# A gated linear attention kernel on one core: later loads for the third group, w_in's upper half in two units, and another order of the steps around two groups

## Chip, core and metric

The kernel runs on one core of one Trainium2 chip. The metric is the device time of one execution in microseconds (us). Before the change it was 279.6 us, the median of three runs (279.18 to 279.66). The engines are called PE (TensorE), DVE (VectorE), ACT (ScalarE), POOL (GpSimd) and SP (SyncE, which here only issues DMAs).

## What is computed

There are two parts, one behind the other. The first is a recurrence for each of 4 batches and 8 heads, over 768 positions, with a 48 x 48 state that decays row by row:

```
state = alpha[t][:, None] * state + outer(k[t], v[t])
y[t]  = q[t] @ state
```

The 8 heads side by side give x (4 x 768 x 384). The second part projects x with w_in (384 x 1024) into a value half and a gate half, runs a first-order scan over the positions on the value half (`h = a * h + val[t]`, with a from A_log), multiplies it by silu of the gate, and projects with w_out (512 x 384) to the output. The weights and A_log come as 64-bit floats and are converted on the core; all the rest is float32.

## The kernel before

The work is cut into 12 groups of 256 positions: 4 batches of 3 groups. A group of the recurrence is called m here, as in the code, and a group of the second part n; in the loop over n the second part of group n runs beside the recurrence of group m = n + 1, and DVE prepares group n + 2 or later. Everything is under a manual schedule: each engine runs its instructions in the order of the program text, waits by semaphores where it needs another's result, and nothing is moved by a planner. So the order of calls in the loop is the order on every engine.

For one group of the recurrence:

- `load_raw`, `load_steps` (L401, L418) load q, k and alpha, `load_v` (L431) loads v. All loads behind the first ones are issued on SP's queue, in order. For the first four groups `load_steps` uses one half of a buffer per group; from then on `load_raw` fills the whole buffer.
- The inputs are turned so that positions run along the free axis. For the first groups PE does it (`turned`, L684: by matmuls with an identity or, for k and q of group 1 and alpha of group 3, by transposes) and ACT copies the result (`alphas`, `straighten`). From group 4 on DVE does it by `turn` (L594).
- DVE forms running products of alpha, P (`scan_P`, L625) and V (`scan_V`, L642), and from them Zk and Zq (`scaled_k`, L609; `scaled_q`, L602). From group 4 on these steps are a generator, `products` (L656): turn of alpha, P, turn of k, V, Zk, turn of q, Zq, seven steps; `go(count)` in the loop runs the next `count` of them.
- `first(m)` is `scores` (L733: 64 small matmuls of Zk with Zq on PE) and `masks` (L748: DVE masks one half of the result into A, ACT copies the other into AK, from group 3 on POOL masks AK).
- `second(m)` is `values` (L766) and `states` (L795) on PE, and `add_up` (L820), which adds the states up on POOL; for the first groups `add_banks` (L832) does it on DVE.
- `third(m)` is `carried` (L782) and `values` again on PE, and `join` (L900): ACT copies y and DMAs bring it into the layout xT of the second part.

For one group of the second part, `project(n, cc)` (L915) is called for cc = 0 to 3: six matmul calls into two PSUM banks, first the value half, then the gate half; the scan over positions on DVE; silu on ACT; and a function that multiplies both (on DVE for n < 2, on POOL later). `output(n)` (L945) multiplies by w_out, ACT copies the result (L950) into one of two buffers, and SP stores it. PSUM banks for `project`, `output` and half of `scores` are taken in turn from four, in pairs, so that each pair is used again two calls later.

The weights: `load_w` (L451) loads a unit of w_in's column blocks, `low(i)` (L539) and `convert(i)` (L546) bring block i into float32 with one step on ACT, two on DVE and one on POOL; blocks 4 and 5 are the halves of w_out. `units` (L447) has three units: block 0, block 1, and blocks 2 and 3 together.

The opening (L962 to L1029) runs group 0 and issues the loads. At L1001 POOL writes one element of the alpha buffer; the load of alpha for group 2 behind it must wait for that write, and so must all SP issues after it. Then follow the unit of blocks 2 and 3, k and q of group 2, alpha of group 3, v of group 1, w_out and v of group 2.

Of the kernel before, what the change touches and what calls it, by code (L numbers as in the profile page):

```python
# [346 lines left out]
def fast(  # L347
# [96 lines left out]
    w_ins = [const.tile([C, NK, 2, C], FP32, name=f"w_in{i}") for i in range(NI)]  # L444
    NW = 6
    UW = NK * 2 * C
    units = [range(0, 1), range(1, 2), range(2, 4)]  # L447
    wbits = {us: const.tile([C, NK, 2, len(us) * C, 2], U32, name=f"wbits{us.start}") for us in units}
    wobits = [const.tile([C, 2, DM, 2], U32, name=f"wobits{i}") for i in range(2)]

# [225 lines left out]
    def bank(tag=None):  # L676
        if tag:
            return ps_at.tile([C, 512], FP32, tag=tag, name=tag)
        return ps_mm.tile([C, 512], FP32, tag="mm", name="mm")
# [1 line left out]
    def bank_pair(tag=None):  # L681
        return [bank(tag and f"{tag}{i}") for i in range(2)]

    def turned(m, name, js, t):  # L684
        raw = steps_of(name, m)
        tp = t[:, 0:len(js) * C].rearrange("p (j x) -> p j x", j=len(js))
        if (m, name) in ((1, "k"), (1, "q"), (3, "a")):
            for n, j in enumerate(js):
                nc.tensor.transpose(tp[:, n], raw[:, ds(ROW + j * D - 64, C)], ident)  # L689
                nc.tensor.transpose(tp[0:64, n], raw[:, ds(j * D, 64)], ident)  # L690
            return tp.rearrange("p j (c h) -> p h c j", h=4)
        for n, j in enumerate(js):
            for i in range(2):
                nc.tensor.matmul(tp[ds(64 * i, 64), n], raw[:, ds(i * ROW + j * D, 64)], ident,  # L694
                                 start=True, stop=True, skip_group_check=True)
        return tp.rearrange("p j (c h) -> p h c j", h=4)

    def copy_turned(to, js, tp, engine=None):
        place = by_runs(to)[:, :, :, js.start:js.stop]
        if engine:  # L700
            return engine.tensor_copy(out=place, in_=tp)
        return nc.scalar.activation(place, tp, AF.Copy)

    def turn_over(m, name, to, tags=(None, None)):
        size = NJ // len(tags)
        copies = []
        for n, tag in enumerate(tags):
            js = range(size * n, size * (n + 1))
            copy = copy_turned(to, js, turned(m, name, js, bank(tag)), nc.vector if n % 2 and tag else None)
            if tag:  # L710
                for other in copies[(n + 1) % 2::2]:
                    tc.declare_no_dep(copy.ins, other.ins, reason="the copies write different steps")
                copies.append(copy)
# [198 lines left out]
    prev_h = [None] * NI  # L912
    fs = {}

    def project(n, cc, late=False):  # L915
        if cc == 0:
            if n == 0:
                fs[n] = [wide[:, k // 2, ds(k % 2 * GC, GC)] for k in range(NI)]
            else:
                fs[n] = [f_last[:, k] for k in range(NI)]  # L920
        xT = xTs[n]
        pv, pg = [t[:, 0:GC] for t in bank_pair()]
        order = [(vg, kk) for vg in range(2) for kk in range(NK)]
        if n == 0 and cc == 0:
            order.sort(key=lambda x: x[1])
        for vg, kk in order:
            nc.tensor.matmul((pv, pg)[vg], w_ins[cc][:, kk, vg, :], xT[:, kk, :],  # L927
                             start=(kk == 0), stop=(kk == NK - 1))
        hh = p2.tile([C, GC], FP32, tag=f"h{cc}", name="hh")

        def scan():
            nc.vector.tensor_tensor_scan(  # L932
                out=hh, data0=a_dec[:, cc:cc + 1].to_broadcast([C, GC]), data1=pv,
                initial=prev_h[cc][:, GC - 1:GC] if n % NG else 0.0, op0=ALU.mult, op1=ALU.add)
            prev_h[cc] = hh

        if not late:
            scan()
        sg = p2.tile([C, GC], FP32, tag="sg", name="sg")
        nc.scalar.activation(sg, pg, AF.Silu)  # L940
        engine = nc.vector if n < 2 or n == N - 1 else nc.gpsimd
        f = lambda: engine.tensor_mul(fs[n][cc], sg, hh)  # L942
        return (scan, f) if late else f
# [34 lines left out]
    def go(count):  # L978
        for _ in range(count):
            next(steps, None)  # L980
# [17 lines left out]
    low(0)  # L998
    parts = [turned(1, "q", js, bank()) for js in halves]
    convert(0)  # L1000
    nc.gpsimd.memset(raws["a"][0:1, 0:1], 0.0)  # L1001
    load_steps("a", 2, [nc.sync])
    load_w(units[2], nc.sync)
    masks(0)
    low(1)
    first_values(True)
# [6 lines left out]
    last = P[:, :, GC]  # L1013
    nc.scalar.activation(ratio[:, 0], last, AF.Copy, scale=1.0 / FIRST_PRODUCT)
    nc.scalar.activation(lower[:, :, 0], last, AF.Copy)
    for name in "kqa":
        load_steps(name, 2 + (name == "a"), [nc.sync])
    load_v(1, nc.sync)
    P = scan_P(1)
    first_carried((1,))  # L1020
# [2 lines left out]
    first_join()  # L1023
    nc.scalar.activation(a_dec, a_log, AF.Exp)
    nc.scalar.activation(spare, minus, AF.Silu)
    for half in range(2):
        load_w_out(half, nc.sync)
    load_v(2, nc.sync)
    junk(0)  # L1029

# [11 lines left out]
    def third(m):  # L1042
        if m < N:
# [4 lines left out]
            if m >= NG:  # L1048
                add_up(m, (3,))

    for n in range(N):
        m = n + 1
        if n == 0:
            V = scan_V(1, P)
            f0 = project(n, 0)
            scaled_k(1, tk, V)
            scaled_q(1, tq, P)
            low(2)
            f1 = project(n, 1)
            convert(2)  # L1060
            alphas(2)
            low(3)
            first(m)
            f0()
            f1()
            tk = straighten(2, "k")
            load_raw("k", 3, nc.sync)
            P = scan_P(2)
            tq = straighten(2, "q")
            V = scan_V(2, P)  # L1070
            convert(3)
            junk(1)
            low(4)
            f2 = project(n, 2)
            values(m, True)
            st = states(m)
            add_banks(m, st)
            alphas(3)
            third(m)
            for name in "qa":  # L1080
                load_raw(name, 3 + (name == "a"), nc.sync)
            load_v(3, nc.sync)
            for c in range(G):
                scaled_k(2, tk, V, c)
                scaled_q(2, tq, P, c)
        elif n == 1:
            scores(m)
            h3, f3 = project(0, 3, True)
            masks(m)
            f2()  # L1090
            P = scan_P(3)
            h3()
            values(m, True)
            st = states(m)
            add_banks(m, st)
# [24 lines left out]
            scaled_q(3, tq, P)  # L1120
            f3()
            go(1)
        else:
            if n == 2:
                first(m)
                go(1)
                f0 = project(n, 0)
                second(m)
                go(2)
            else:  # L1130
                second(m)
                go(4)
                f0 = project(n, 0)
            f0()
            load_raw("k", n + 3, nc.sync)
            load_raw("a", n + 3, nc.sync)
            go(1)
            f1 = project(n, 1)
            f1()
            if n == N - 2:  # L1140
                for i in range(0, 2):
                    check_w(i)
            go(1)
            f2 = project(n, 2)
            f2()
            load_raw("q", n + 3, nc.sync)
            if n == N - 2:
                check_w(2)
            if n == N - 1:
                check_flag()  # L1150
            go(1)
            f3 = project(n, 3)
            f3()
            third(m)
            first(m + 1)
            load_v(m + 2, nc.sync)
        if n == N - 2:
            for i in range(3, NW):
                check_w(i)
            check_end()  # L1160
        if n == N - 1:
            tc.mark_branch_hint_location("last", hint=0, engines=[mybir.EngineType.PE, mybir.EngineType.Activation, mybir.EngineType.DVE, mybir.EngineType.SP, mybir.EngineType.Pool])
            value = nc.values_load(flag[0:1, 0:1], min_val=0, max_val=1)
        if 0 < n < N - 1:
            output(n)
    return value


# [59 lines left out]
```

## Time and profile before

| | |
|---|---|
| runs | 279.6, 279.66, 279.18 us |
| the profiled execution | 279.43 us, span 277.7 us |
| granted TensorE clock | 1.0 |
| PE, DVE, POOL, ACT busy | 268.8, 218.3, 122.4, 108.6 us |
| share of PE in the chain that ended last | 92% |
| DMA | 41.18 MB, mean 148 GB/s |

The profiled execution is one run of its own, and the terms of a sum taken from its rows are to be set against its 279.43 us. "Busy" is the time in which an engine had an instruction running. The chain that ended last is found by going back from the last instruction, at each step to what released it; what is on it set the end, and what is not on it had time to spare. In a row of the timeline the first number is the start in us from the begin of the span, the second the length; what stands in brackets behind it is the idle time of the engine before it and the instruction that ended it. L numbers are lines of the kernel.

### The profile page before, as it was taken

Reading aid. Unit: us, or ns where it says so; the run is one execution under the profiler, and the core shown is the slowest. Engines: PE = TensorE matmul, PEld = TensorE weight load, DVE = VectorE, ACT = ScalarE, POOL = GpSimd, SP = SyncE. Lnnn points to the kernel's source line nnn. Section 1 sums busy time; section 2 is a strip of 40 time slices with the busy share of each in tenths; the row PEclk is TensorE's granted clock in tenths of the full one; section 3 lists DMA queues with packets and bytes.
Section 4 is the critical chain, followed back from the end, with each engine's and each line's share of the span. In section 5 each row is a group of like instructions: output and inputs, shape, how many; then the busy total and the mean of one; then the engine's idle time right before and its main releaser. Section 6 shows DMA issues by size and latency. Waiting matters only on the chain.

```text
span 277.7 us, 9598 instructions
## 1 busy us (share of the span) xinstructions
PE 268.8 (97%) x4056; PEld 217.0 (78%) x4056; DVE 218.3 (79%) x281; ACT 108.6 (39%) x244; POOL 122.4 (44%) x141
## 2 busy tenths in 40 slices
PE   7999999999989999899999999999999999999995
PEld 5988887876678688488688688688688688787874
DVE  7979998898798995995895995996995993079540
ACT  2577763461332532341542433433434425213111
POOL 8141223130068574563473584484384476435000
PEclk9999999999999999999999999999999999999999
DMA  6949993845919777487468587576687501201201
GB/s 196 295 140 309 296 262 78 205 88 139 267 48 238 149 199 182 103 214 163 103 181 199 114 205 164 130 197 155 152 186 159 144 0 27 77 1 33 71 5 59
DMA packets 51599, 41.18 MB, mean 148 GB/s; under 512 B 27360, under 2 KB 49536, under 8 KB 51552
## 3 DMA queue, kind: packets, MB, share of 16 engines
q1 hardware_dynamic: 48752, 37.50, 53.1%
q0 software_dynamic: 1408, 2.03, 2.8%
q10 hardware_dynamic: 1392, 0.99, 1.2%
q8 instruction: 33, 0.54, 0.9%
q14 instruction: 14, 0.11, 0.2%
HBM read 32.54 MB, written 4.72 MB: 134 GB/s over the span
## 4 chain that ended last, share of the span: by engine, by line
PE 92%; DVE 3%; DMA 1%; POOL 1%; issue 1%; ACT 1%; SPq 0%; DVEq 0%; ACTq 0%
PE mm L927 45%; PE mm L956 21%; PE y L791 4%; PE y L778 4%; PE mm L744 3%; PE s L744 3%; PE s L810 3%; PE mm L694 2%; PE mm L1189 2%; DMA raw_a<-in_alpha_dram 1%; POOL AK L762 1%; DVE P L630 1%; DVE V L649 1%; PE mm L689 1%; PE y L862 1%
## 5 line engine op out<-in xcount | busy, mean ns | idle before, releaser
L927 PE MATMUL mm<-xT,w_in 128*128 128x256 f32 x576 | 128.9, 382 | 0.6 <-ACT xT L884 0.6
L927 PEld LDWEIGHTS mm<-xT,w_in 128*128 128x128 f32 x576 | 108.1, 190 | 16.3 <-issue 0.8
L956 PE MATMUL mm<-w_out,f_last 128*128 128x384 f32 x160 | 54.1, 492 | 1.3 <-DVE A L759 1.3
L940 ACT ACTIVATE sg<-mm 128x256 f32<-128x256 f32 x48 | 18.4, 384 | 85.8 <-PE mm L927 80.3
L956 PEld LDWEIGHTS mm<-w_out,f_last 128*128 128x128 f32 x160 | 29.7, 190 | 21.1 <-issue 1.4
L830 POOL TENSOR_TENSOR sum<-sum,dS 128x192 f32<-128x192 f32 x30 | 33.2, 1108 | 27.3 <-PE mm L927 13.5
L942 POOL TENSOR_TENSOR f_last<-sg,hh 128x256 f32<-128x256 f32 x36 | 30.9, 862 | 30.6 <-ACT sg L940 23.1
L932 DVE TENSOR_TENSOR_SCAN hh<-a_dec,hh,mm 128x256 f32<-128x256 f32 x32 | 23.4, 732 | 15.4 <-PE mm L927 15.2
L630 DVE TENSOR_TENSOR_SCAN P<-al,lower 128x1028 f32<-128x1028 f32 x12 | 31.1, 2595 | 0.6
L649 DVE TENSOR_TENSOR_SCAN V<-al,ends 128x1028 f32<-128x1028 f32 x12 | 28.3, 2356 | 0.4
L907 POOL DMA_DIRECT2D xT<-yst x40 | 20.5, 517 | 13.1 <-ACT yst L904 11.8
L950 ACT ACTIVATE o_sb<-mm 128x384 f32<-128x384 f32 x22 | 10.8, 491 | 38.4 <-PE mm L956 38.4
L762 POOL TENSOR_TENSOR AK<-AK,mask 128x512 f32<-128x512 f32 x9 | 13.2, 1464 | 17.2 <-ACT AK L760 17.2
L759 DVE TENSOR_TENSOR A<-s,mask 128x256 f32<-128x256 f32 x9 | 3.8, 425 | 21.5 <-PE s L744 21.5
L557 POOL TENSOR_TENSOR w_in<-w_in,wr 128x768 int32<-128x768 int32 x4 | 7.3, 1826 | 26.0 <-DVE wr L555 17.0
L595 DVE STREAM_TRANSPOSE k<-raw_k 128x1024 f32<-128x1024 f32 x9 | 18.3, 2033 | 0.0
L595 DVE STREAM_TRANSPOSE q<-raw_q 128x1024 f32<-128x1024 f32 x9 | 18.2, 2022 | 0.0
L778 PEld LDWEIGHTS y<-AK,v 64*64 64x64 f32 x352 | 12.1, 134 | 6.4 <-issue 5.0
L595 DVE STREAM_TRANSPOSE al<-raw_a 128x1024 f32<-128x1024 f32 x8 | 16.3, 2041 | 0.1
L778 PE MATMUL y<-AK,v 64*64 64x64 f32 x352 | 14.5, 221 | 1.0 <-POOL AK L762 1.0
L791 PEld LDWEIGHTS y<-Zq,sum 48*64 48x64 f32 x656 | 11.8, 134 | 4.3 <-issue 4.1
L791 PE MATMUL y<-Zq,sum 48*64 48x64 f32 x656 | 14.4, 221 | 0.6 <-issue 0.6
(158 smaller groups left out, 392.2 us busy)
## 6 DMA issues: line engine op xcount, KB each, us to landing
v<-in_v_dram SPq DMA_DIRECT2D x22, 192.0 KB, 3.3
out_dram<-o_sb SPq DMA_DIRECT2D x22, 192.0 KB, 2.1
raw_k<-in_k_dram SPq DMA_DIRECT2D x18, 184.0 KB, 3.4
raw_q<-in_q_dram SPq DMA_DIRECT2D x18, 184.0 KB, 3.8
raw_k<-in_k_dram SPq DMA_DIRECT2D x18, 176.0 KB, 3.8
raw_q<-in_q_dram SPq DMA_DIRECT2D x18, 176.0 KB, 4.1
raw_a<-in_alpha_dram SPq DMA_DIRECT2D x16, 184.0 KB, 5.0
raw_a<-in_alpha_dram SPq DMA_DIRECT2D x16, 176.0 KB, 5.1
```

Of the source, the lines that this page charges most:

```text
L595: nc.vector.transpose(out=by_runs(to).rearrange("p h c j -> p h j c"), in_=raws[name][:, 0:4 * ROW].rearrange("p (h j d) -> p h j d", h=4, ...
L630: nc.vector.tensor_tensor_scan(out=P, data0=al[:, 0:4 * GP], data1=lower.rearrange("p h t -> p (h t)"), initial=0.0, op0=ALU.mult, op1=ALU ...
L649: nc.vector.tensor_tensor_scan(out=V[:, ::-1], data0=al[:, 1:4 * GP + 1][:, ::-1], data1=ends.rearrange("p h t -> p (h t)")[:, ::-1], init ...
L778: nc.tensor.matmul(ys[m][i][ds(64 * s, 64), e, ds(c * C + h * L, L)], v_sb[rows, c, 4 * i + p, :], As[i][rows, c, p, :], start=across and ...
L791: nc.tensor.matmul(ys[m][i][ds(64 * s, 64), e, ds(u * L, L)], Ss[j][rows, p, :], Zqs[m % 2][rows, u, p, D:], start=False, stop=True, skip_ ...
L830: nc.gpsimd.tensor_add(Ss[j][:, :, 0:D], Ss[j - 1][:, :, 0:D], part)
L907: engines[n % len(engines)].dma_start(out=xT[to, a], in_=st[rows, i, e])
L927: nc.tensor.matmul((pv, pg)[vg], w_ins[cc][:, kk, vg, :], xT[:, kk, :], start=(kk == 0), stop=(kk == NK - 1))
L932: nc.vector.tensor_tensor_scan(out=hh, data0=a_dec[:, cc:cc + 1].to_broadcast([C, GC]), data1=pv, initial=prev_h[cc][:, GC - 1:GC] if n % ...
L940: nc.scalar.activation(sg, pg, AF.Silu)
L942: f = lambda: engine.tensor_mul(fs[n][cc], sg, hh)
L956: nc.tensor.matmul(os[c], fs[n][cc][:, ds(c * C, C)], w_outs[cc // 2][:, cc % 2, :], start=(cc == 0), stop=(cc == NI - 1))
```

## The change

In words:

- w_in's blocks 2 and 3 are two units, each with its own load. The load of block 3 comes behind the k, q and alpha loads that followed.
- The write that holds alpha of group 2 is made by ACT and reads `wide_S[2]`, behind the last small copies of the opening, and not by POOL; the loads behind it move there as well.
- w_out is no longer loaded in the opening but in the loop's first pass, behind `third(1)`, and there k of group 3 is loaded too, which was loaded before behind its own turn. `low(3)` moves down, and `low(4)` is made by `convert(4)`.
- In the first pass `project(0, 2)` takes a function `between`: the value half's matmuls, the scan, then `values` and `states` of group 1 with their sums, then the gate half.
- The second half of alpha for group 3 is turned by matmuls and not by transposes.
- For the groups in `late`, 1 and 3: `first(5)` is called behind `output(3)`, not before it, and `second(3)` and `second(5)` are called behind `project(n, 1)`. At n = 4 the steps of `products` are spread 2, 2, 1, 2, where they were 4, 1, 1, 1, and k and alpha are loaded behind `project(4, 1)`. The load of q moves behind the following step of `products` in all passes.

```diff
-    units = [range(0, 1), range(1, 2), range(2, 4)]
+    units = [range(i, i + 1) for i in range(NI)]
...
-    def turned(m, name, js, t):
+    def turned(m, name, js, t, by_transpose=None):
...
-        if (m, name) in ((1, "k"), (1, "q"), (3, "a")):
+        if (m, name) in ((1, "k"), (1, "q"), (3, "a")) if by_transpose is None else by_transpose:
...
-            copy = copy_turned(to, js, turned(m, name, js, bank(tag)), nc.vector if n % 2 and tag else None)
+            copy = copy_turned(to, js, turned(m, name, js, bank(tag), False if (m, name, n) == (3, "a", 1) else None), nc.vector if n % 2 and tag else None)
...
-    def project(n, cc, late=False):
+    def project(n, cc, late=False, between=None):
...
+        passes(order[:NK] if between else order)
...
         if not late:
             scan()
+        if between:
+            between()
+            passes(order[NK:])
...
-    nc.gpsimd.memset(raws["a"][0:1, 0:1], 0.0)
-    load_steps("a", 2, [nc.sync])
-    load_w(units[2], nc.sync)
...
     nc.scalar.activation(lower[:, :, 0], last, AF.Copy)
+    nc.scalar.activation(raws["a"][0:1, 0:1], wide_S[2][0:1, D:D + 1], AF.Copy)
+    load_steps("a", 2, [nc.sync])
+    load_w(units[2], nc.sync)
     for name in "kqa":
         load_steps(name, 2 + (name == "a"), [nc.sync])
+    load_w(units[3], nc.sync)
     load_v(1, nc.sync)
...
-    for half in range(2):
-        load_w_out(half, nc.sync)
     load_v(2, nc.sync)
...
+    late = (1, 3)
     for n in range(N):
...
-            low(3)
             first(m)
             f0()
             f1()
             tk = straighten(2, "k")
-            load_raw("k", 3, nc.sync)
             P = scan_P(2)
             tq = straighten(2, "q")
             V = scan_V(2, P)
+            low(3)
             convert(3)
             junk(1)
-            low(4)
-            f2 = project(n, 2)
-            values(m, True)
-            st = states(m)
-            add_banks(m, st)
+            def across_and_states():
+                values(m, True)
+                add_banks(m, states(m))
+
+            f2 = project(n, 2, between=across_and_states)
             alphas(3)
             third(m)
-            for name in "qa":
+            for half in range(2):
+                load_w_out(half, nc.sync)
+            for name in "kqa":
                 load_raw(name, 3 + (name == "a"), nc.sync)
...
             if n == 2:
                 first(m)
-                go(1)
-                f0 = project(n, 0)
-                second(m)
-                go(2)
-            else:
+            if n - 1 not in late:
                 second(m)
                 go(4)
-                f0 = project(n, 0)
+            else:
+                go(n // 2)
+            f0 = project(n, 0)
             f0()
-            load_raw("k", n + 3, nc.sync)
-            load_raw("a", n + 3, nc.sync)
-            go(1)
+            if n == 2:
+                go(2)
+            if n != 4:
+                load_raw("k", n + 3, nc.sync)
+                load_raw("a", n + 3, nc.sync)
+                go(1)
             f1 = project(n, 1)
             f1()
+            if n - 1 in late:
+                second(m)
+            if n == 4:
+                go(2)
+                load_raw("k", n + 3, nc.sync)
+                load_raw("a", n + 3, nc.sync)
...
             f2 = project(n, 2)
             f2()
-            load_raw("q", n + 3, nc.sync)
...
-            go(1)
+            go(2 if n == 4 else 1)
+            load_raw("q", n + 3, nc.sync)
             f3 = project(n, 3)
             f3()
             third(m)
-            first(m + 1)
+            if n not in late:
+                first(m + 1)
             load_v(m + 2, nc.sync)
...
             output(n)
+        if n > 1 and n in late:
+            first(m + 1)
```

More of the change, by code (lines that the diff above doesn't have):

```diff
@@ L925, in project, with passes @@
             order.sort(key=lambda x: x[1])
-        for vg, kk in order:
-            nc.tensor.matmul((pv, pg)[vg], w_ins[cc][:, kk, vg, :], xT[:, kk, :],
-                             start=(kk == 0), stop=(kk == NK - 1))
+        def passes(part):
+            for vg, kk in part:
+                nc.tensor.matmul((pv, pg)[vg], w_ins[cc][:, kk, vg, :], xT[:, kk, :],
+                                 start=(kk == 0), stop=(kk == NK - 1))
+        passes(order[:NK] if between else order)
         hh = p2.tile([C, GC], FP32, tag=f"h{cc}", name="hh")
```

## Prediction

> **What bounds the kernel now.** I read the page first, then the waits of PE (TensorE's matmuls), then the chain, then the timelines of DVE, POOL, ACT and SP around each gap.
>
> ```profile
> PE 268.8 (97%) x4056; PEld 217.0 (78%) x4056; DVE 218.3 (79%) x281; ACT 108.6 (39%) x244; POOL 122.4 (44%) x141
> q8 instruction: 33, 0.54, 0.9%
> PE y L778 <- POOL AK L762: 1.0, 1, 1.0
> ```
>
> PE is busy 97% of the span, so an edit pays only where PE stands still. Behind the opening its waits name a gap of 1.0 us, and the chain (start, length, what) shows one of 0.65 and one of 1.2, from 111.63 to 112.81. Together that is 2.9 us of 279.43 (the profiled execution; its span is 277.7), the most this change can earn there.
>
> ```profile
> 41.96 0.11 PE mm L690
> 42.07 0.39 PE y L791 x16
> ...
> 43.50 0.65 issue
> 44.15 0.39 PE y L791 x10
> 44.54 0.76 PE s L744 x30
> ```
>
> ```profile
> 108.46 0.39 PE y L791 x16
> ...
> 110.02 0.77 PE s L744 x32
> 110.79 0.84 PE mm L744 x32
> 111.63 0.42 DVE A L759
> 112.05 0.77 issue
> 112.81 5.40 PE mm L956 x16
> ```
>
> The gaps at 43.50 and after 111.63 have no engine behind them: other output steps start without waiting for that mask, and "issue" means that nothing in the profile held PE. Both follow PE's densest stretch, `third` (96 small matmuls from 108.46 to 110.02) and `scores` (64 to 111.63): with their weight loads 320 instructions in 3.2 us. PE's queue q8 brought 33 packets for 2 x 4056 instructions, about 250 a packet; such a stretch eats a packet faster than the next arrives. I take both for late instruction packets.
>
> **The change, part by part.**
>
> *n = 0, `between` and the half of alphas(3) by plain matmuls.* values(1) and states(1) move between the two halves of project(0,2), so half a projection stands between the dense states and alphas(3), and 16 instructions are added. From 42.07 to 44.54 third(1) took 2.47 us; undisturbed it takes 110.02 - 108.46 = 1.56. Gain 0.9. What bounds it, and what is late next:
>
> ```profile
> 28.81 1.90 PE mm L694 x32
> 36.05 2.79 PE mm L927 x12
> 43.64 0.69 DVE L605 TENSOR_TENSOR Zq<-q,P 128x512 f32<-128x512 f32 x1
> ```
>
> A projection takes 2.79, so the packet gets half of that, 1.4 us, more than the 0.9 it was late. Next is Zq(2): its second half ends at 44.33, and the second half of scores(2) would begin at 44.4: no more than 0.9 can be had. The matmul form of a full turn took 1.90 (first row); the form by transposes is 16 steps of 0.11 (the row of 41.96), 1.8 at least. Half of the difference, 0.05, is the swap's cost at most. **-0.9** (-0.95 to 0).
>
> *The loads held longer, w_in in four units.* One ACT write, last of three small ones, replaces the POOL memset; a(2) goes out behind it instead of at 19.32:
>
> ```profile
> 19.32 1.19 SPq L421 DMA_DIRECT2D raw_a<-in_alpha_dram  x2
> 21.18 0.22 ACT L1015 ACTIVATE lower<-P 128x4 f32<-128x4 f32 x1
> 28.57 1.08 ACT L544 ACTIVATE wr<-wbits 128x768 uint16<-128x768 uint32 x1 [1.23 <-DMA wbits<-in_moe_w_in_dram]
> wbits<-in_moe_w_in_dram SPq DMA_DIRECT2D x2, 768.0 KB, 6.3
> GB/s 196 295 140 309 296 262 78 205 88 139 267 48 238 149 199 182 103 214 163 103 181 199 114 205 164 130 197 155 152 186 159 144 0 27 77 1 33 71 5 59
> ```
>
> Issued at about 21.6, 2.3 us later, and at worst the 6.3 us to landing of the larger weights: a(2) is there by 27.9 and PE wants it at 28.8 (row above): hidden. low(2) waited until 28.57 for both upper slices, two DMAs of 768 KB; now half of that stands ahead of it. At 296 to 309 GB/s (the page's slices from 20.8 to 34.7) 0.79 MB less are 2.6 us, which pays for the 2.3. Nothing gained or lost (at the ends, -0 and +1, if a(2) lands after 28.8).
>
> *w_out and k(3) behind third(1) on SP.* They are queued behind join(1) and ahead of k(4), join(2) and the stores of output(0):
>
> ```profile
> 45.19 3.15 SPq L907 DMA_DIRECT2D xT<-yst  x4
> 54.01 0.54 DVE L553 TENSOR_SCALAR w_out<-wobits 128x768 uint32<-128x768 uint32 x1
> 58.88 2.04 DVE L595 STREAM_TRANSPOSE k<-raw_k 128x1024 f32<-128x1024 f32 x1
> 69.42 1.20 SPq L951 DMA_DIRECT2D out_dram<-o_sb  x2
> 72.92 0.49 ACT L950 ACTIVATE o_sb<-mm 128x384 f32<-128x384 f32 x1 [4.18 <-PE mm L956]
> wobits<-in_moe_w_out_dram SPq DMA_DIRECT2D x2, 768.0 KB, 7.4
> ```
>
> join(1) leaves SP at 48.34, 0.9 earlier after the gain: w_out is issued from 47.4 and lands within 7.4, by 54.8 at worst; the slice of 41.7 to 48.6 moved only 78 GB/s, and without k(3) it is emptier, so I take 53 to 54, against a need at 54.01 for the second half. k(3), 0.74 MB later, lands at 56 to 58 against 58.88. Both just fit. What I expect to slip is further back: some 2.3 MB more pass SP's queue before k(4), and the stores of output(0), issued at 69.42, go by 0 to 1.5 us later. ACT's copy at 72.92 reuses their buffers, now wanted at 72.0, and project(2,0) needs the banks that it empties. **+0.5** (0 to +1.5).
>
> *n = 2, second(3) behind project(2,1).* The 1.0 us wait for POOL's mask goes:
>
> ```profile
> 78.97 0.27 PE L778 MATMUL y<-AK,v 64*64 64x64 f32 x2 [1.01 <-POOL AK L762]
> 84.23 0.73 DVE L932 TENSOR_TENSOR_SCAN hh<-a_dec,hh,mm 128x256 f32<-128x256 f32 x1
> 80.38 7.97 PE mm L927 x36
> ```
>
> The wait began at 78.0. PE now runs project(2,1) there (7.97 / 3 = 2.66) to 80.6, second(3) (80.38 - 78.97 = 1.4) to 82.0 and project(2,2) to 84.7. project(2,3) then needs the banks of project(2,1), whose scan ends at 84.96: a new wait of 0.3. On POOL the product f1, which needs that scan, now stands ahead of the sums of step 3; they start after 85, and the last could reach `third` up to 0.9 late. I take none of that, since third(3) begins at 87.6 with other work. **-0.7** (-1.0 to +0.2).
>
> *n = 3 to 4, first(5) behind output(3).* This breaks the dense stretch, so 111.63 to 112.81, 1.2 us, goes. But DVE runs in program order, and its masks of step 5 stand ahead of its whole work for step 6:
>
> ```profile
> 111.61 0.42 DVE L759 TENSOR_TENSOR A<-mm,mask 128x256 f32<-128x256 f32 x1 [0.34 <-PE mm L744]
> ...
> 114.29 2.74 DVE L630 TENSOR_TENSOR_SCAN P<-al,lower 128x1028 f32<-128x1028 f32 x1
> ...
> 126.98 1.20 DVE L605 TENSOR_TENSOR Zq<-q,P 128x1024 f32<-128x1024 f32 x1
> 131.65 0.77 PE s L744 x32
> 75.56 2.29 DVE L630 TENSOR_TENSOR_SCAN P<-al,lower 128x1028 f32<-128x1028 f32 x1
> ```
>
> From the end of the mask, 112.03, to the end of Zq(6), 128.18, DVE had 16.15 us without a pause; with P at 2.29, 15.7, and 15.3 if the small steps beside POOL shrink too. scores(6) needs Zq(6). Counted from the end of third(4): before, scores(6) began 131.65 - 110.02 = 21.6 later. After: output(3) 5.4, scores(5) 1.55, mask 0.4, DVE 15.3 to 15.7, together 22.6 to 23.0. PE's own path, output(3) to scores(6) as before, 131.65 - 112.81 = 18.8, and scores(5), 1.55, together 20.4, arrives 2.2 to 2.6 us early and waits. The gap of 1.2 is exchanged for a larger one. **+1.2** (+1.0 to +1.5).
>
> *The rest.* From n = 5 the order is that of before; q's load moves behind one DVE step in SP's program order, with nothing between: nothing. At n = 4 the loads of k(7) and a(7) wait for the turn of k(6): a(7) lands some 2 us before its turn.
>
> Sum: -0.9 + 0.5 - 0.7 + 1.2 = +0.1. The profiled execution, 279.43, lies 0.17 under the median of 279.6; on the median **279.7**.
>
> **Rivals.**
>
> - *DVE does not bind at n = 4* (it gains on PE where I see no slack). For it: DVE is busy only 79% on the page. Against: it has to, within these 23 us. Then -0.9 - 0.7 - 1.2: 276.8. Chance 0.08.
> - *The stores do not slip and all gains come in full*: -0.95 - 1.0 + 1.0, about 278.7. Chance 0.14.
> - *Slower: the late loads.* The place is convert(5) on DVE, in order ahead of scan, turn of k(3) and everything of step 3. It decides when w_out's second half lands after 54.5 or k(3) after 59.4; each us past that is a us on PE, since project(1,3) needs the scan behind them, and the stores slip as well: +1 to +2, 281.2. Chance 0.17.
> - *Slower: a third late packet.* 16 more instructions move every packet edge by 16 for the rest of the run; where a packet falls into the next such dense stretch (n = 5 and on), 0.65 to 1.2 more: 280.6. Chance 0.13. The Trainium skill, "Advanced Engine Details and Errata", section ISA Cache, gives lines of 256 instructions and only two of them; by that rule the next packet is asked for no earlier than one packet ahead, as both gaps of this trace, 0.65 and 1.2, suggest.
> - *The change doesn't do what it says: the "issue" gaps are no late packets*, and 0.65 at n = 0 stays: 0.9 of the sum is lost, 280.6. Chance 0.06. The Trainium skill, "Runtime: NRT & Kernel Launch", section Instruction fetch mechanics, says this for it: the next page is fetched while the present one runs, and crossing is mostly hidden. The two gaps speak against it.
>
> **How the numbers follow.** The forecast, 279.7, has chance 0.42, with a range of its own from 279.1 to 280.2. About 0.2% (0.56 us) is what a measurement of this kernel can tell from no change. Faster by more: 0.08 + 0.14 = 0.22. Within: 0.42. Slower: 0.17 + 0.13 + 0.06 = 0.36. The range leaves out the first rival and the far end of the late loads: 278.4 to 281.3.
>
> **What would show it.** Right: no "issue" gap in third(1); no wait of PE for the mask AK of step 3, a few tenths before project(2,3); about 2.5 us of PE's idle time before scores(6), at some 131 us, released by DVE's Zq. Wrong: PE reaching scores(6) without that wait, DVE waiting for wbits, wobits or raw_k near 54 to 59, ACT waiting for a DMA before the copy of output(1), or a new "issue" gap behind n = 4.

## The result, and the profile after

The changed kernel takes **287.97 us** (median of 6 runs, 285.62 to 290.68) against 279.55 (6 runs, 279.18 to 279.66): ratio 1.0281, 95% interval 1.0231 to 1.0331. The ratio leaves out the run of 290.68, which was disturbed. 279.7 was forecast, with a range up to 281.3: in place of no change that can be measured there is a loss of 8 us. The profiled execution of the changed kernel took 286.17 us (span 284.5) against 279.43 (277.7), so 6.74 us have to be found in the traces. It is one of the two shortest runs: these two have a mean clock of 0.993, and the three of 287.13 to 288.94 have 0.982.

The page of the changed kernel: PE's row, and the granted clock in 40 slices.

```profile
PE 271.5 (95%) x4064; PEld 218.8 (77%) x4064; DVE 218.5 (77%) x281; ACT 108.4 (38%) x245; POOL 117.8 (41%) x140
...
PEclk9999999999979999999999999999999999999999
```

PE is busy 2.7 us longer than before for 8 more matmuls: part of the loss is not a wait but slower matmuls, in the one slice where the clock row shows a 7 (the row gives the TensorE clock that was granted, in tenths of full speed). PE's waits in the same run (total, times, longest):

```profile
PE mm L928 <- ACT o_sb L956: 4.5, 1, 4.5
PE s L744 <- DVE Zq L605: 2.8, 1, 2.8
```

The second wait was forecast (2.2 to 2.6), the first was not. Neither the mask AK nor an "issue" gap is left in the list. The chain around the first wait (start, length, what):

```profile
73.59 5.28 DMA out_dram<-o_sb
...
78.97 0.50 ACT o_sb L956
79.47 0.04 issue
79.51 6.91 PE mm L928 x24
...
87.77 5.38 PE mm L928 x24
```

PE is ready for project(2,0) 4.5 us before 79.51, at 75.0: output(0)'s stores are issued at 73.59, not at 69.42 as before, and take 5.28 to land; only then may ACT overwrite their buffer (o_sb) and empty the bank. The 24 matmuls behind the wait take 6.91, where 24 like them take 5.38 without one (last row). The windows around it (PE busy, PEld, DVE, ACT, POOL, then granted clock, DMA share, GB/s) say why:

```profile
75.70:79.10 3.40, 0.00 (x0) 0.00 (x0) 2.03 (x1) 0.13 (x1) 0.00 (x0) 1.00 0.93 273
79.10:82.50 3.40, 2.99 (x7) 2.45 (x8) 0.02 (x1) 2.17 (x6) 1.26 (x1) 0.50 0.47 155
82.50:85.90 3.40, 3.40 (x17) 2.99 (x17) 3.31 (x5) 1.51 (x3) 0.74 (x1) 1.00 0.00 0
```

Behind 3.4 us without a matmul the clock is granted at half for the next 3.4 us. This is a second price of the wait, about 1.5 us, and nothing in the prediction paid it. Why the stores are late is on SP, in order (start, length of the issue):

```profile
47.73 1.10 SPq L459 DMA_DIRECT2D wobits<-in_moe_w_out_dram  x2
48.93 2.18 SPq L410 DMA_DIRECT2D raw_k<-in_k_dram  x4
51.21 5.57 SPq L410 DMA_DIRECT2D raw_q<-in_q_dram  x4
57.13 2.81 SPq L410 DMA_DIRECT2D raw_a<-in_alpha_dram  x4
60.43 1.90 SPq L440 DMA_DIRECT2D v<-in_v_dram  x2
62.43 4.39 SPq L410 DMA_DIRECT2D raw_k<-in_k_dram  x4
66.92 5.32 SPq L907 DMA_DIRECT2D xT<-yst  x8
...
73.59 1.25 SPq L957 DMA_DIRECT2D out_dram<-o_sb  x2
```

Before, these four parts of the queue read:

```profile
48.44 1.96 SPq L410 DMA_DIRECT2D raw_q<-in_q_dram  x4
50.49 2.86 SPq L410 DMA_DIRECT2D raw_a<-in_alpha_dram  x4
53.45 1.01 SPq L440 DMA_DIRECT2D v<-in_v_dram  x2
60.94 1.75 SPq L410 DMA_DIRECT2D raw_k<-in_k_dram  x4
```

The reader is to see two things. Before, SP stood idle from 54.46 to 60.94, until DVE had turned k(3) and its buffer came free for k(4); that is 6.5 us of room. Now SP is busy to 62.33, and k(4) starts 1.5 later. But 1.0 of this would come on an idle queue too: DVE's turn of k(3) ends at 61.92, not at 60.92, behind a wait of 2.48 for w_out's second half. And the same issue of four DMAs takes 4.39 instead of 1.75, that of q 5.57 instead of 1.96. 1.5 + 2.6 is nearly the whole slip of the stores, 4.2. For q, SP's own waits list 3.8 us that end with the landing of w_out, a wait that is not in the list of before. What holds k(4)'s issue the profile does not name. Both long issues stand where the DMA engines are full, as the same windows of both kernels show:

```profile
54.00:62.00 8.00, 8.00 (x124) 6.45 (x123) 5.52 (x6) 6.53 (x12) 3.62 (x2) 1.00 1.09 222
62.00:70.00 8.00, 8.00 (x31) 5.44 (x30) 7.81 (x11) 1.36 (x3) 0.00 (x0) 1.00 0.96 195
```

```profile
54.00:62.00 8.00, 8.00 (x124) 6.44 (x123) 7.96 (x9) 5.89 (x12) 3.84 (x2) 1.00 0.59 111
62.00:70.00 8.00, 8.00 (x30) 5.51 (x29) 6.72 (x9) 1.37 (x3) 0.00 (x0) 1.00 0.60 141
```

DMA share 1.09 and 0.96 after (first fence), 0.59 and 0.60 before (second); a packet's whole time counts in the window in which it starts, so a share can pass 1.

The other wait, from DVE's timeline of the changed kernel (idle time before in brackets):

```profile
121.16 0.42 DVE L759 TENSOR_TENSOR A<-s,mask 128x256 f32<-128x256 f32 x1 [8.46 <-PE s L744]
121.92 0.42 DVE L759 TENSOR_TENSOR A<-mm,mask 128x256 f32<-128x256 f32 x1 [0.34 <-PE mm L744]
...
136.92 1.22 DVE L605 TENSOR_TENSOR Zq<-q,P 128x1024 f32<-128x1024 f32 x1
```

and from its chain:

```profile
138.29 1.00 PE s L744 x32
```

DVE idles 8.46 us for the scores of step 5, then does its whole work for step 6 (15.8 us from the end of the second mask, 122.34, to the end of Zq, 138.14), and PE gets Zq(6) at 138.29. PE has no other wait on this stretch. In this execution no half clock follows the wait: it falls into two of the clock's windows, and PE works 1.80 of 3.41 us in the first and 2.24 in the second.

From point to point (starts on PE, before and after): first project 23.39 and 24.04; output(0) 60.4 and 60.28; output(1) 68.15 and 68.03; output(2) 91.14 and 95.93; scores(6) 131.65 and 138.29. So +0.65 in the opening (the same 16 matmuls at 4.7 us take 1.97 and not 1.56: the clock records of the trace grant full speed from 7.42 there, and from 5.78 before; in all the traces of this case this start lies between 4.4 and 7.6, so it is not of the change), -0.8 in the first pass, +4.9 between output(1) and output(2), +1.85 to scores(6), +0.1 behind it.

### The profile page after: what moved, and what is told of

It reads as the page before. It is cut to its first block, busy times and chain, and to the rows that moved or that the text cites. A ratio compares the mean times of both kernels' runs of the same rounds, so it can differ in the third digit from the quotient of the medians.

```text
span 284.5 us, 9615 instructions
## 1 busy us (share of the span) xinstructions
PE 271.5 (95%) x4064; PEld 218.8 (77%) x4064; DVE 218.5 (77%) x281; ACT 108.4 (38%) x245; POOL 117.8 (41%) x140
## 4 chain that ended last, share of the span: by engine, by line
PE 87%; DVE 6%; DMA 3%; issue 1%; ACT 1%; DVEq 0%; SPq 0%; ACTq 0%
PE mm L928 43%; PE mm L962 21%; PE y L778 4%; PE y L791 4%; PE mm L744 3%; PE s L744 3%; PE s L810 3%; PE mm L694 2%; DMA out_dram<-o_sb 2%; PE mm L1206 2%; DVE V L649 2%; DMA raw_a<-in_alpha_dram 1%; DVE P L630 1%; DVE Zk L614 1%; DVE hh L935 1%
## 5 line engine op out<-in xcount | busy, mean ns | idle before, releaser
L928 PE MATMUL mm<-xT,w_in 128*128 128x256 f32 x576 | 130.9, 385 | 5.0 <-ACT o_sb L956 4.5
L948 POOL TENSOR_TENSOR f_last<-sg,hh 128x256 f32<-128x256 f32 x36 | 33.4, 932 | 40.8 <-DVE hh L935 20.7
L830 POOL TENSOR_TENSOR sum<-sum,dS 128x192 f32<-128x192 f32 x30 | 32.1, 1070 | 22.1 <-ACT dS L818 12.1
L762 POOL TENSOR_TENSOR AK<-AK,mask 128x512 f32<-128x512 f32 x9 | 11.4, 1272 | 25.5 <-ACT AK L760 25.4
L614 DVE TENSOR_TENSOR Zk<-k,V 128x1024 f32<-128x1024 f32 (+1 forms) x14 | 15.2, 1085 | 0.1
L605 DVE TENSOR_TENSOR Zq<-q,P 128x1024 f32<-128x1024 f32 (+1 forms) x14 | 14.8, 1057 | 0.1
```

The source lines that it names most:

```text
L614: nc.vector.tensor_mul(Zks[m][:, ds(c0, n)].rearrange("p c h t -> p h c t"), t[:, :, at].rearrange("p h (c t) -> p h c t", t=C), V[:, :, 1 ...
L830: nc.gpsimd.tensor_add(Ss[j][:, :, 0:D], Ss[j - 1][:, :, 0:D], part)
```

## The experiments

Theory after the result: **two waits make the loss, each with a stretch of slow clock behind it** (behind the second only in some executions); the first comes from late loads that hold up the stores, the second from DVE's order. Rivals: another part of the change holds up the stores (the held loads, POOL's or ACT's order); the slow clock has a cause of its own; the gains that were forecast never came. "Before" in each group is the kernel before, run again on the chip of the group: median 279.72 in the first group of four, 279.33 in the second, 279.43 in the third, 279.62 in the last.

**The kernel before with all late loads** (held loads, w_in in four units, w_out and k(3) behind third(1)), none of the new order:

```diff
+    nc.scalar.activation(raws["a"][0:1, 0:1], wide_S[2][0:1, D:D + 1], AF.Copy)
+    load_steps("a", 2, [nc.sync])
...
             third(m)
-            for name in "qa":
+            for half in range(2):
+                load_w_out(half, nc.sync)
+            for name in "kqa":
```

> The kernel before with the later loads alone: a(2) and all behind it held by the ACT write, w_in's upper half as two units, w_out and k(3) behind third(1); no between, no new order of first and second. Theory A (SP's queue: the stores of output(0) go out some 4 us later behind w_out, k(3), q(3), a(4), so ACT waits before it empties output(1) and PE before project(2,0)): about 279.5 + 4 to 6 = 283.5 to 285.5, with a wait of PE for ACT's o_sb near 75. Theory B (the hand-over at n = 3 to 4 is the main loss): 279.5 to 280. Theory C (the later loads starve DVE at convert(5), from which all later steps slip): 281 to 282, without that wait of PE.

Measured 283.42 (282.13 to 284.49), ratio 1.0158 (1.0125 to 1.0192); a wait of 3.3 for o_sb, and half clock for 3.4 us behind it. So the loads alone bring the first wait. SP's rows show that the room on its queue was not used up:

```profile
59.27 1.17 SPq L440 DMA_DIRECT2D v<-in_v_dram  x2
61.23 4.51 SPq L410 DMA_DIRECT2D raw_k<-in_k_dram  x4
...
72.50 1.27 SPq L951 DMA_DIRECT2D out_dram<-o_sb  x2
```

SP is through at 60.44 and waits for k(4)'s buffer, which DVE frees at 61.20. k(4) starts only 0.3 later than before; its issue takes 2.8 longer, and that is the slip of the stores, 3.1. Not expected: the gap of 0.65 at n = 0 is gone, though nothing stands between the states and alphas(3).

**The changed kernel, output(0)'s stores on ACT's queue:**

```diff
-            nc.sync.dma_start(out=out[b, ds(g * GC + c * C, C), :], in_=o_sb)
+            (nc.sync if n else nc.scalar).dma_start(out=out[b, ds(g * GC + c * C, C), :], in_=o_sb)
```

> The changed kernel with the two stores of output(0) issued on ACT's queue right behind the copies, not on SP's. Theory A (only the place in SP's queue is late): ACT's wait before output(1) goes, and with it PE's 4.5 us and the slow clock behind it, 1.5 us: about 281 to 282. Theory A' (the 16 DMA engines are full, so the stores land late whatever queue issues them): less than 2 us better, 285 to 288.

Measured 283.47 (282.29 to 284.49), ratio 1.0159 (1.0117 to 1.0201). That is between the two forecasts. The wait for o_sb is gone, the 2.8 before scores(6) is left, with half clock behind it from 134.1 to 137.5. A wait of 1.1 for xT of join(2) is new, and the edit brings it: SP issues k(4) only at 66.59, behind a wait of 4.9 that ends with the landing of the first moved store, so join(2) leaves SP 1.5 later than in the changed kernel. On ACT's queue the stores go at 64.63 and land in 1.9: it was their place in SP's queue that made them late.

**The changed kernel with w_out loaded in the opening as before:**

```diff
     nc.scalar.activation(spare, minus, AF.Silu)
+    for half in range(2):
+        load_w_out(half, nc.sync)
     load_v(2, nc.sync)
```

> The changed kernel with the loads of w_out back in the opening; k(3) stays behind third(1). Theory A: 1.57 MB less stand ahead of the stores of output(0), about 5 us at 300 GB/s, more than the 4.2 by which they came late: the wait of PE is gone or below 1 us, 280.5 to 282. If k(3) alone is enough to delay the stores: 284 or more.

Measured 283.28 (282.51 to 284.36), ratio 1.0136 (1.0093 to 1.0179). No wait for o_sb; the 2.8 before scores(6) stays. It is dearer than the 280.5 to 282 expected, since half clock follows this wait too: from 132.55 to 139.37, two windows, in the profiled run.

**The changed kernel with first(5), second(5) and n = 4 as before** (`late = (1,)`, steps 4, 1, 1, 1):

> The changed kernel with late = (1,): first(5) ahead of output(3) again, n = 4 in the order of before; second(3) still behind project(2,1). Theory of the prediction (DVE's work for step 6 stands behind first(5)): the waits of 0.7 and 2.8 us at n = 4 go, the packet gap of up to 1.2 us may come back: 1 to 2 us faster than the changed kernel, 285 to 287. If the hand-over were the main loss: 281.

Measured 284.05 (282.55 to 286.36), ratio 1.0183 (1.0117 to 1.0249). The wait before scores(6) is gone, that for o_sb is 3.6, and an "issue" gap of 1.3 is back behind third(4). The wait of 0.7 at n = 4 that the expectation names is in no row of PE, in the changed kernel either. The two waits are independent: either one alone leaves the kernel some 4 us over before, although the gains at n = 0 and n = 2 are in.

**The kernel before with `between` alone:**

```diff
+            def across_and_states():
+                values(m, True)
+                add_banks(m, states(m))
+
-            f2 = project(n, 2)
-            values(m, True)
...
+            f2 = project(n, 2, between=across_and_states)
```

> The kernel before with the argument between alone: the sums of group 1 stand between the halves of project(0,2); every load, the form of alphas(3) and all of n > 0 are as before, so the k(3) and v loads are still in flight at 39 to 47 us. Theory A (the gap of 0.65 in third(1) is a packet that arrives late because the stretch is dense): half a projection in between covers it, third(1) falls from 2.47 to about 1.6, 278.8 to 279.0 in all. Theory B (the packet is late because it shares the DMA engines with k(3) and v, which the kernel with late loads alone lacked there): it is late wherever PE needs it, a gap of about 0.6 stays in project(0,2) or in third(1), 279.5 to 279.8.

Measured 278.56 (277.98 to 280.46), ratio 0.9974 (0.9950 to 0.9998). No gap in third(1), at a DMA share of 0.76 from 39 to 46 us (0.49 before): with half a projection in between the gap is gone even when the DMA engines are busier. That is as Theory A says; but the kernel with late loads lost the gap with nothing in between, so neither A nor B is the whole.

**w_out in the opening, and first(5) back** (both edits from above):

> The changed kernel with w_out loaded in the opening again, and n = 4 and first(5) as before: what is left of the change is the held loads, between, k(3) behind third(1) and second(3) behind project(2,1). Theory (the two waits, each with the slow clock behind it, are the whole loss): no wait of 2.8 before scores(6), no wait for o_sb, clock 1.0 throughout; -0.7 at n = 0 and -0.7 to -1.0 at n = 2, 278.0 to 278.6, plus up to 0.65 if the opening falls badly against the clock's windows. Rival (something else in the order of n = 0 to 2 costs as well): 279.6 or more.

Measured 280.4 (277.97 to 286.31), ratio 1.0013 (0.9982 to 1.0045): 278.0 to 278.6 was expected. Neither wait is left, yet it gains nothing. Its chain and its windows:

```profile
110.53 1.65 issue
...
112.60 7.05 PE mm L962 x16
```

```profile
110.00:113.40 3.40, 1.75 (x35) 1.20 (x28) 1.19 (x3) 2.22 (x7) 2.76 (x6) 1.00 0.31 85
113.40:116.80 3.40, 3.40 (x7) 1.75 (x6) 3.35 (x3) 0.27 (x2) 1.18 (x1) 0.50 0.62 124
```

The gap behind third(4) is 1.65, and it also brings the half clock: output(3)'s 16 matmuls take 7.05 and not 5.36. A window in which PE works 1.75 of 3.40 us was enough here. It does not happen each time: runs with a clock of 1.0 took 277.97 to 280.14, those with 0.994 280.16 to 281.83, and one with 0.982 took 286.31.

**w_out in the opening, and DVE's turn of alpha(6) and P(6) ahead of first(5)** (the lines that move DVE's steps; go(2) at the head of n = 4 goes):

```diff
         if n > 1 and n in late:
+            go(2)
             first(m + 1)
```

> The changed kernel with w_out loaded in the opening again, and the turn of alpha and P of group 6 placed on DVE ahead of the masks of first(5), which stays behind output(3). Theory (DVE's order is the cause of the wait of 2.8: its work for step 6 stands behind masks(5), for which it idles 8.46 us): DVE uses that idle time, Zq(6) is ready some 5 us earlier, no wait before scores(6), clock 1.0, and the packet gap of 1.2 behind third(4) stays away: 277.0 to 278.2. Rival (DVE's work for step 6 is bound by its loads or by POOL beside it, not by the order): a wait of 1 to 3 us stays, 281 to 283.

Measured 279.47 (278.47 to 280.67), ratio 1.0008 (0.9986 to 1.0030). The wait falls from 2.8 to 1.3 and the clock stays at 1.0; Zq(6) still ends late, at 131.53, since the turn of k(6) waits behind a scan. (The profile puts this wait down to ACT's copy of y, which ends within 0.02 us of Zq(6); scores elsewhere, as at 110.02 before, start right behind `third` without it.) The time lies between the two forecasts, the direction is the theory's. A gap of 0.4 came back in third(1), in spite of `between`.

**The changed kernel with idle matmuls in both waits:** 9 ahead of project(2,0) and 6 ahead of scores(6), on an empty bank, read by nothing (the first of the two):

```diff
+            if n == 2:
+                warm("y0", 9)
             f0 = project(n, 0)
```

> The changed kernel with 9 matmuls without use on an empty bank ahead of project(2,0) and 6 ahead of scores(6), which run while PE would wait for o_sb and for Zq; nothing reads them. Theory (each of the two waits costs a window at half clock on top of itself, some 1.7 us each): the waits' ends stay, the clock is 1.0 throughout, 284 to 285.5, and the runs lie closer together than the 5 us of the changed kernel. Rival (the clock falls for another reason than PE's idleness, or the waits alone make the loss): 287 to 289, clock 0.98 to 0.99 as before.

Measured 287.9 (287.38 to 288.44), ratio 1.0292 (1.0271 to 1.0312). By the time the rival would seem right, and the trace says otherwise (L733 are the idle matmuls):

```profile
75.61 4.08 PE y L733 x18
79.69 5.18 PE mm L934 x24
...
199.38 1.67 issue
201.04 0.40 PE mm L750 x2
201.45 7.05 PE mm L968 x16
```

project(2,0) starts where it did, to 0.2 us, and the 24 matmuls take 5.18, not 6.91: **1.7 us for the slow clock, shown by taking away PE's idleness alone** (1.5 against the 5.38 that 24 take elsewhere). PE starts scores(6) at 136.81, not at 138.29. But at n = 8 there is a gap of 1.67, where the changed kernel has none, and half a clock behind it. The kernel has 30 more matmul instructions ahead of it; that they moved a late packet there is likely and not shown. All four runs have a clock of 0.994 and lie within 1.1 us, where those of the changed kernel at 0.993 and 0.982 lie 3.3 apart.

**The kernel before with `between` and second(3) behind project(2,1), no load moved:**

```diff
+            f1()
+            if n == 2:
+                second(m)
```

> The kernel before with between in project(0,2) and second(3) behind project(2,1); every load and the rest of the order as before. Theory (these two steps of the change do what they are for, and the losses come from the loads and from n = 4): no wait for POOL's AK, no wait for o_sb, 278.56 (with between alone) less 0.7 to 1.0, 277.5 to 277.9. Rival (the wait for the mask only moves, to the banks that project(2,3) needs or to third(3)): 278.3 to 278.8.

Measured 278.41 (277.61 to 280.76), ratio 0.9974 (0.9943 to 1.0005). 277.5 to 277.9 was expected. From output(1) to output(2) PE takes 22.11 us in the chain (67.65 to 89.76), against 22.89 with `between` alone (67.95 to 90.84): -0.78. But behind third(4) PE stands still for 1.3 us here and stood for 0.7 there, and three of the twelve runs, of 279.9 to 280.76, have a clock of 0.994; so both come out at a ratio of 0.9974.

**The same, with first(5) behind output(3), second(5) behind project(4,1), three DVE steps ahead of first(5) and V right behind its masks:**

```diff
+            elif n == 4:
+                go(1)
...
+        if n == 3:
+            go(3)
+            first(m + 1)
```

> The kernel of the run before in this call, and first(5) behind output(3) and second(5) behind project(4,1) as in the change, but with three of DVE's steps for group 6 (turn of alpha, P, turn of k) ahead of the masks of first(5) and V right behind them. Theory (DVE's order alone makes the wait before scores(6); with two steps ahead 1.3 us of it were left, and the turn of k takes 2.0): no wait before scores(6), clock 1.0, and the dense stretch behind third(4) is broken up: 277.0 to 277.9, 0 to 0.6 under the run before. Rival (the wait stays, since DVE's work is bound otherwise): 278.5 to 280.

Measured **277.34** (276.61 to 277.84), ratio **0.9927** (0.9905 to 0.9950), faster than both kernels. Its timeline of DVE, and its chain:

```profile
111.57 2.01 DVE L595 STREAM_TRANSPOSE k<-raw_k 128x1024 f32<-128x1024 f32 x1
115.28 0.42 DVE L759 TENSOR_TENSOR A<-s,mask 128x256 f32<-128x256 f32 x1 [1.70 <-PE s L744]
...
127.02 1.23 DVE L605 TENSOR_TENSOR Zq<-q,P 128x1024 f32<-128x1024 f32 x1
```

```profile
128.94 0.70 PE y L791 x48
129.64 0.77 PE s L744 x32
```

DVE idles 1.70 and not 8.46 before the masks, Zq(6) ends at 128.25, and scores(6) follows third(5) without a wait. Behind the opening no "issue" gap over 0.25 us is left, and none of the six runs shows a clock under 0.999. DVE's order was the cause of the wait.

**The kernel before, w_out alone late:**

```diff
             third(m)
+            for half in range(2):
+                load_w_out(half, nc.sync)
             for name in "qa":
```

> The kernel before with w_out's loads alone moved behind third(1); k(3), the held loads and w_in's unit of two as before. Theory (w_out's 1.57 MB on SP's queue between join(1) and the stores are the cause): the stores of output(0) leave some 3 us late, PE waits 2.5 to 4 for o_sb at project(2,0) and loses up to a window at half clock: 282 to 284. Rival (it takes k(3) and the held loads as well, which the kernel with all late loads had): no wait for o_sb over 0.5, 279 to 280.

Measured 279.12 (278.11 to 281.1), ratio 1.0003 (0.9980 to 1.0026). My theory falls: w_out alone costs nothing. SP's rows:

```profile
55.74 1.18 SPq L440 DMA_DIRECT2D v<-in_v_dram  x2
60.97 1.75 SPq L410 DMA_DIRECT2D raw_k<-in_k_dram  x4
...
69.45 1.18 SPq L951 DMA_DIRECT2D out_dram<-o_sb  x2
```

SP is through at 56.92 and still waits to 60.97 for k(4)'s buffer. By then the DMA engines have caught up: their share is 1.03 from 54 to 62 us, but 0.58 from 62 to 70, and k(4) takes its 1.75. The stores go at 69.45, as before.

**The kernel before, k(3) alone late** (`for name in "kqa"` behind third(1)):

> The kernel before with k(3)'s load alone moved behind third(1). Theory (the gap of 0.65 in third(1) comes with the loads of k(3) and v that are in flight then): with 0.74 MB less in flight it shrinks to 0 to 0.4, and k(3) behind join(1) and ahead of w_in's rest costs nothing: 278.8 to 279.3. Rival (the packet is late by its place in the dense stretch alone): the gap stays, 279.3 to 279.9.

Measured 278.74 (278.09 to 279.21), ratio 0.9983 (0.9968 to 0.9999). It costs nothing either, and third(1) runs undisturbed in its old order, from 42.31 to 43.87, at a DMA share of 0.08 from 39 to 46 us.

**The kernel before, w_out and k(3) late, nothing held:**

> The kernel before with w_out and k(3) both loaded behind third(1), and nothing else; each alone cost nothing, since SP's queue was idle from 56.4 to 56.9 until k(4)'s buffer came free at 60.4 to 61.0. Theory (the two together use up this idle time and fill the DMA engines): k(4) is issued at 61 to 62 and takes over 4 us to issue, the stores of output(0) leave at 72 or later, PE waits 2.5 to 4.5 for o_sb, 282.5 to 284.5 as with all late loads. Rival (the held loads and w_in's two units are needed as well): stores at 69 to 70, no wait for o_sb over 0.5, 278.5 to 279.5.

Measured 283.83 (283.57 to 284.73), ratio 1.0154 (1.0120 to 1.0188), the time of all late loads together. Its waits and its SP:

```profile
PE mm L927 <- ACT o_sb L950: 4.3, 1, 4.3
```

```profile
61.70 1.01 SPq L440 DMA_DIRECT2D v<-in_v_dram  x2
62.80 4.78 SPq L410 DMA_DIRECT2D raw_k<-in_k_dram  x4
...
74.30 1.02 SPq L951 DMA_DIRECT2D out_dram<-o_sb  x2
```

**Both together are needed, and enough**: two edits that cost nothing one by one cost 4.2 us together. The held loads take no part. With both the DMA share is 1.09 from 54 to 62 us and 0.98 from 62 to 70. The stores slip by 4.9: 1.9 in k(4)'s start (DVE's turn of k(3) ends 1.7 later, so an idle queue would have saved little) and 3.0 in the length of its issue. So the two loads together seem to use up the time of the DMA engines rather than the idle time of SP's queue; in the kernel with all late loads SP even waited, and the stores slipped all the same.

**The changed kernel with k(3) where it was:**

> The changed kernel with k(3)'s load back behind its own turn, where it was before; w_out stays behind third(1). Theory (either of the two may be late, not both): no wait for o_sb, stores of output(0) at 69 to 70; the wait of 2.8 before scores(6) and the slow clock behind it stay: 282.5 to 284, as with w_out back in the opening. Rival (any of the late loads is enough once the rest of the change is there): the wait for o_sb stays at 2 or more, 285 to 289.

Measured 283.09 (281.95 to 283.33), ratio 1.0125 (1.0097 to 1.0153): the wait for o_sb is gone, the stores go at 70.23, the 2.8 before scores(6) is left. Taking back either load removes the first wait.

## Why the prediction was wrong

- *n = 0, -0.9.* Right in what it gains: third(1) is undisturbed in the changed kernel (42.92 to 44.48, 1.56 as forecast). PE's path from the first project to scores(2) gained 0.71: the projection in two halves takes twice 1.49 and not 2.79, 0.2 that I left out. The reason given, a packet that is late because the stretch is dense, is not the whole and not shown: without `between` the gap goes too when k(3) or w_out is loaded later (DMA share 0.02 to 0.08 from 39 to 46 us), and with `between` 0.4 of it came back in one kernel, at a share of 0.63.
- *The loads held longer, 0.* Right: without them the loss is the same.
- *w_out and k(3) behind third(1) on SP, +0.5 (0 to +1.5).* **This step failed.** It said that "the stores of output(0), issued at 69.42, go by 0 to 1.5 us later". They go 4.2 later and land in 5.3, PE waits 4.5, and a half clock follows that costs 1.5 to 1.7, a term that the sum did not have at all. The two loads alone cost 4.2. I counted the moved bytes for landing times and took the issues at their lengths from an empty queue. The trace before had the row that speaks against it: k(3)'s issue at 34.69 took 5.80, behind w_out and v, where k(4)'s takes 1.75. An estimate from its rows: w_out is 1.57 MB and k(3) 0.74; at the 296 to 309 GB/s of the busy slices they need some 5.2 and 2.5 us, and the room up to k(4) is 6.5: each alone fits, both don't. This is no proof: at the 222 GB/s that the full window of the changed kernel moved, w_out alone would need 7.1, and it cost nothing.
- *n = 2, -0.7.* Right: -0.78. The wait of 0.3 before project(2,3) did not come; scores(4) starts after a pause of 0.07, and its first half takes 1.00, not 0.77.
- *n = 3 to 4, +1.2 (1.0 to 1.5).* The mechanism was right, the size was off: +1.85. The wait is 2.8 (2.2 to 2.6 forecast), as DVE takes 15.8 from mask to Zq and not 15.3 to 15.7, and PE's own path is 0.25 longer than before. **The slow clock was left out here as well.** It is not in the profile of the changed kernel, but behind the same wait the clock is 0.5 from 133.1 to 136.5 with k(3) back and from 132.55 to 139.37 with w_out back. These two kernels, which have this wait alone, lie 3.5 and 3.6 us over before in spite of the gains.
- *Rivals.* The late loads (0.17) had the direction. Their point was reached: w_out's second half lands at some 56.4 and DVE waits 2.48 for it. But that cost PE nothing; output(0) starts at 60.28. The stores, mentioned there in half a sentence, did it; that they would not slip is refuted. A third "issue" gap did not come in the changed kernel, but in the one with idle matmuls, at 1.67 plus the clock. That DVE doesn't bind is refuted.
- *The markers.* "ACT waiting for a DMA before the copy of output(1)" was named as a sign of being wrong, and it is what the trace shows.

What remains open: the "issue" gaps sit where late packets of instructions would, come and go with what stands between, with DMA load and with the count of instructions, but no run took the packets themselves away. And why a single issue on SP takes 3 to 4 us, as the first of k(4)'s four DMAs does, stays open too: it goes with full DMA engines in these traces, but no run changed their load and nothing else.

## What to carry to other kernels

Before loads are moved on an in-order queue, find the first transfer behind them that an engine needs. Ask how much idle time the queue has up to it, and whether the DMA engines will still be at work on all the moved loads together when its turn comes. Edits that are free one by one can share one slack. An issue that takes three times its usual length in the trace is a sign that the transfers behind it will be late. Price each new wait of PE of more than a microsecond or two with the slow clock behind it, and when a consumer is moved later on an engine, move other work ahead of it, or all of that engine's later work moves too.

## What the runs showed of the hardware

The clock falls to half in windows of 3.41 us (79.10 to 82.51 in the changed kernel), whose place against the program changes from run to run; one window costs 1.5 to 1.7 us here. The Trainium skill, "TensorE: Matmul & The Clock Gate", Part 1: The HAM clock gate, has the same window (3413 ns, free-running). Its section on HAM oscillation warns of idle gaps over some 3.4 us; here gaps of 1.65 and 1.67 were enough, in windows with PE busy 1.75 of 3.40 and 1.73 of 3.40. In these traces PE's busy time in a window tells more than the length of one gap: the wait of 2.78 in the profile of the changed kernel, spread over two windows with PE busy 1.80 and 2.24 of 3.41, brought no half clock, and a gap of 1.28 in the kernel with `between` and second(3) brought none in the profiled run. One window does not fit: with w_out back in the opening the half clock stayed for a second window although PE was busy 2.84 of 3.41 in the first.

The length of an issue of four DMAs on SP ranged from 1.73 us to 6.96, and whatever stands behind it on SP's queue waits as long. k(4)'s took 1.75 at a DMA share of 0.31 during the issue (before) and of 0.54 (w_out alone late), and 4.39 to 4.78 at 0.92 to 1.00 in the changed kernel and in the two others with both loads late.
